# Sliding-window attention and a two-layer ELU network on one core: batch 1's queries and keys transposed in other portions and other steps

## The chip, the cores and the metric

The kernel runs on one core of a Trainium2 chip. The metric is the device time of one execution in microseconds (us). A core has five engines with a queue each, which work side by side and meet at semaphores: TensorE (PE, with its weight loads as PEld), VectorE (DVE), ScalarE (ACT), GpSimd (POOL) and SyncE (SP). POOL, SP and ACT also issue transfers to the DMA engines. TensorE writes its results to PSUM, a buffer of eight banks, from which DVE and ACT read them.

## The reference

Attention over 8 batches, 8 heads, 576 tokens and a head size of 64, in which a token sees only the tokens at most 32 away; then a network of two layers on the 4,608 tokens with 512 values each:

```python
scores = scale * np.matmul(q, k.transpose(0, 1, 3, 2))
scores = np.where(np.abs(pos[:, None] - pos[None, :]) <= 32, scores, -1e9)
attn = np.exp(scores - max); attn = attn / (sum(attn) + 1e-9)
x = np.matmul(attn, v)          # to (B*S, H*D) = (4608, 512)
h = x @ w_in                    # 512 x 2048
g = np.where(h > 0, h, np.exp(np.minimum(h, 0)) - 1)
out = g @ w_out                 # 2048 x 512, float32
```

## The kernel before

**The network's steps set the beat.** The 4,608 tokens are 18 tiles `t` of 256 tokens, and the 2,048 inner values are eight groups of 256, so there are 144 steps `kk`. The first 16 steps take tiles 0 and 1 in turn. In step `kk`, `mm1(kk)` makes `h` for one tile and one group: eight matmuls of 256 columns (L734, in the profile `ps`), with PSUM tiles in two banks, `h0` for even steps and `h1` for odd ones. `exponents` then issues the exp on ACT (L744, `e_sb`) and `subtract` the minus one on DVE (L756, `m_sb`). `elu(kk)`, issued on DVE at the start of step `kk + 1`, makes `g_sb` out of `ps` and `m_sb` (L767) and so frees the bank for step `kk + 2`. `mm2(n)` adds `g_sb` times `w_out` to the sums of a tile (four matmuls of 512 columns, L787, `psY`), for `n = kk - 2` in the general case. When a tile's last sums are done, ACT and DVE copy them out as `y_sb` and SP issues their transfer.

**Attention is laid between these by hand.** A dictionary of tasks holds what is issued in a step: `at(kk, slot, fn, ...)` enters it. A step runs its slots in the order "first", the `elu`, "dve", `mm1` (with "half" after its first four matmuls, before the exp is issued), "mid", the `mm2` (a slot with a number `n` runs just before `mm2(n)`), "end". Each engine takes its instructions strictly in the order in which they were issued.

**Pairs.** Attention is done for pairs of blocks of 64 queries, 36 pairs, four and a half to a batch. Pair 4 holds the last block of batch 0 and the first of batch 1; pair 5 is the next two blocks of batch 1, then 6, 7, and pair 8 its last two. `scores` (L384, into `psS`), `exponential` (ACT, L395, `pu`), `mask` (DVE, L404, `pm`), `pv` (L416), `normalize` (DVE, L425 and L428), `x_transpose` (L438) and `x_evac` bring a pair's result to `xT`, which `mm1` of tile `pair // 2` reads. Pair 4's scores come at the end of step 9, pair 5's in step 12, those of 6 and 7 in step 18, of 8 and 9 in step 26.

**Queries and keys must be transposed first**, heads and their 64 values onto the partitions, into `qT` and `kT` (two buffers each, batches in turn). A part of a batch is a pair `(z, nj)`: `32 * nj` tokens from token `z` on. Either `load_cast` brings it as bf16 by a POOL transfer that casts on the way (tile `c`), or `load_qk` brings float32 (tile `f`, SP) and `cast_qk` casts it (L290 on ACT, L292 on DVE, tile `qkb`). `transpose_qk` then transposes it on TensorE into a PSUM tile `ptx`: with `c`, two transposes of half the partitions for each of the `nj` (L335), with `qkb` one (L340); `evict` copies the result to `qT` or `kT`, with strides. From batch 3 on this is done by DMA.

In the kernel before, batch 1 comes in halves of 288 tokens: `HALF_A` by `load_cast`, transposed in steps 8 (queries) and 9 (keys); `HALF_B` by `load_qk`, cast in steps 14 (on ACT) and 15 (on DVE), transposed at the end of steps 15 and 16. The last 64 queries and 32 keys of batch 0 (`FRONT_C`) are transposed in step 6 by `transpose_late`. Batch 2 follows in four groups of nine in steps 22 to 25, which use the PSUM tiles "s" and "u" in turn; each of the two has two banks, and "s" and "u" hold the scores too. `HJ` is 9, `SJ` is 18 and `NC` is 32. ACT's copies of these groups, the casts, the exps and the copies of `xT` and `y_sb` share one queue.

Of the kernel before, what the change touches and what calls it, by code (L numbers as in the profile page):

```python
# [10 lines left out]
BF16 = mybir.dt.bfloat16  # L11
# [10 lines left out]
def kernel(  # L22
# [9 lines left out]
    nc = tc.nc  # L32

    B, H, S, D = q.shape
# [9 lines left out]
    HP = H // 2  # L44
    NC = 128 // HP
# [15 lines left out]
    cpool = ctx.enter_context(tc.tile_pool(name="const", bufs=1))  # L61
# [32 lines left out]
    def ps_tile(shape, dt, tag, name):  # L94
        return pools[tag].tile(shape, dt, tag=tag, name=name)
# [21 lines left out]
    HJ = SJ // 2  # L117
    WHOLE, HALF_A, HALF_B = (0, SJ), (0, HJ), (NC * HJ, HJ)
    FRONT_B = ((NC * HJ, HJ - 2), (NC * HJ, HJ - 1))
    FRONT_C = ((NC * (SJ - 2), 2), (NC * (SJ - 1), 1))  # L120
    qk_f = {}

    def load_qk(b, which, part, engs=(nc.sync, nc.sync)):
        z, nj = part
        mj = max(nj, HJ)
        t = lpool.tile([128, 2, mj * D], FP32, tag=f"f{which}{mj}",
                       name=f"f{which}", bufs=2 if part is WHOLE else 1)
        qk_f[b, which, z] = t
        src = (q, k)[which][b, :, z:z + NC * nj, :].rearrange(
            "(g h) (c j) d -> c g h (j d)", h=2, j=nj)  # L130
        for h in range(2):
            engs[h].dma_start(out=t[:, h, 0:nj * D], in_=src[:, :, h, :])
# [4 lines left out]
    def load_cast(b, which, part):  # L137
        z, nj = part
        mj = nj if nj < 3 else HJ + 1
        t = cpool.tile([128, 2, mj * D], BF16, tag=f"c{which}{mj}",  # L140
                       name=f"c{which}")[:, :, 0:nj * D]
        qk_c[b, which, z] = t
        src = (q, k)[which][b, :, z:z + NC * nj, :].rearrange(
            "(g h) (c j) d -> c g h (j d)", h=2, j=nj)
        nc.gpsimd.dma_start(out=t, in_=src)

    def load_v(b, m, rows=(0, 128)):
        lo = 128 * m - WIN
# [72 lines left out]
    def edges(i):  # L221
# [8 lines left out]
    ident = cpool.tile([128, 128], BF16)  # L230
# [15 lines left out]
        out=far, in_=far, compare_op=ALU.is_ge, fill=FAR,  # L246
# [61 lines left out]
    def keys_or_queries(b, which):  # L308
        if which == 0:
            return qT[b % 2].rearrange("p g s -> p (g s)")  # L310
        return kT[b % 2][:, KPAD:KPAD + HP * S]
# [233 lines left out]

    load_w_in(2, 0, 2)
    for which in range(2):
        load_cast(1, which, HALF_A)
    load_w_in(2, 1, 2)
    load_w_out(2)  # L550
    for m in range(3):
# [4 lines left out]
        load_v(1, m)  # L556
    gate(w_in_at(3))
    for which in range(2):
        load_qk(1, which, HALF_B)
    for which in range(2):  # L560
        load_qk(2, which, WHOLE)

# [5 lines left out]
    def at(kk, slot, fn, *args):  # L568
        tasks.setdefault((kk, slot), []).append((fn, args))
# [19 lines left out]
    at(1, "mid", x_transpose, 3, "y1")  # L589
    at(1, "mid", x_evac, 3, nc.vector)  # L590
    at(5, "dve", swap_pools)
    def transpose_late(tag):
        pt = ps_tile([128, 2, 512], BF16, tag, "ptx")
        evicts = []
        for which in range(2):
            transpose_qk(0, which, FRONT_C[which], 0, FRONT_C[which][1],
                         BOTH[which], later=evicts, pt=pt[:, which, :])
        for evict in evicts:
            evict()

    at(6, "mid", transpose_late, "s")
    at(6, "dve", rotate_back, 0, 3, 4, (1,))

    for which in range(2):
        at(8 + which, (6, "half")[which], transpose_qk, 1, which, HALF_A, 0,
           HJ, nc.scalar, "s")
        at(14 + which, "mid", cast_qk, 1, which, HALF_B, 0, HJ, BOTH[which])
        at(15 + which, "end", transpose_qk, 1, which, HALF_B, 0, HJ,
           nc.scalar, "s")
    at(6, "dve", edges, 2)  # L610
    at(16, "dve", hold_v, 2)
# [32 lines left out]
    for b in range(2, B):  # L644
        k0 = begin[first_pair(b)]


        l_qk, l_v, c0 = {2: (0, 0, 0), 3: (15, 24, 22), 4: (35, 36, 41),
                         5: (52, 52, 57), 6: (68, 68, 73),
                         7: (84, 84, 89)}[b]  # L650
        if b >= 3:
            at(l_qk, "end", load_qk, b, 0, WHOLE)
            at(l_qk, "end", load_qk, b, 1, WHOLE)
            if b > 3:
                at(l_v, "dve", hold_v, b)
            for m in range(VS):
                at(l_v + m, "mid", load_v, b, m)
        if b <= 3:

            if b == 2:  # L660
                at(k0, "dve", rotate_v, b, 0, 1)
            at((21, 28)[b - 2], "mid", rotate_v_dma, b, 3 - b)
        else:
            for n, back in enumerate((10, 8, 3, 2)):
                m0 = 2 * (n // 2)
                at(k0 - back, "dve", rotate_v, b, m0, m0 + 2, (n % 2,))
        if b == 2:

            for n, (which, j0) in enumerate(((0, 0), (0, 9), (1, 0), (1, 9))):
                at((18, 20, 21, 23)[n], ("mid", "end", "end", "mid")[n],  # L670
                   cast_qk, b, which, WHOLE, j0, 9,
                   (nc.vector, nc.scalar, nc.scalar, nc.vector)[n])
                at(22 + n, "end" if n == 1 else "mid", transpose_qk, b, which, WHOLE, j0, 9,
                   nc.scalar, "su"[n % 2])
            continue


        free = [f for f in range(c0, k0) if f not in starts]
        for n, (which, j0) in enumerate(
                (which, j0) for which in range(2) for j0 in (0, 6, 12)):  # L680
            at(free[n], "end", cast_qk, b, which, WHOLE, j0, 6,
               nc.vector if free[n] < 26 else nc.scalar)
            if j0 == 12:
                at(free[n], "end", write_rows, b, which)
                at(free[n] + (3 if free[n] == 29 else 4), "mid",
                   transpose_rows, b, which)
# [72 lines left out]
    def elu(kk, z=0):  # L759
        if z == 0:  # L760
            g_t[kk] = mpool.tile([128, FG, TT], BF16, tag="g_sb", name="g_sb",
                                   bufs=8)
        if kk == 0:
            subtract(kk, z)
        ps = psH[kk][z]
        w = ps.shape[1]
        nc.vector.scalar_tensor_tensor(  # L767
            g_t[kk][:, z * w:(z + 1) * w, :], ps, 0.0, m_t.pop((kk, z)),
            ALU.max, ALU.min)
# [69 lines left out]

    for kk in range(NSTEP):  # L840
        run(kk, "first")
        for n in {1: (), 2: (0, 1)}.get(kk, (kk - 1,)):
            if n >= 0:
                elu(n)
        run(kk, "dve")
        mm1(kk)
        run(kk, "mid")
        if kk == NSTEP - 1:
            last_sums()
        elif kk >= LATE + LAG:  # L850
            for _ in range(3 if kk < LATE + LAG + 4 else 4):
                add(*todo.pop(0))
        else:
            for n in {2: (), 3: (), 4: (), 5: (0, 2), 6: (1, 3), 7: (4,),
                      8: (5, 6)}.get(kk, (kk - LAG,) if kk >= LAG else ()):
                run(kk, n)
                mm2(n)
        run(kk, "end")
# [30 lines left out]
```

## Time and profile before

| what | value |
|---|---|
| three runs | 301.69, 302.32, 302.68 us; median 302.32 |
| the profiled execution | 302.52 us, of which span 300.8 us |
| TensorE's granted clock | 0.999 |
| TensorE busy | 97% of the span |
| DVE, ACT, POOL busy | 80%, 57%, 18% |
| DMA moved | 52.68 MB, 175 GB/s in the mean |
| step 6, products start | 23.87 us |
| step 10, products start | 35.05 us |
| step 19, products start | 54.52 us |
| step 26, products start | 69.92 us |

The span runs from the first instruction to the last; what the time has beyond it lies around the execution. Times within the profile count from the start of the span. In a timeline a matmul's length holds its way through the array, so lengths of matmuls that follow each other overlap; the distance of their starts is what they cost. A steady step takes 1.74 us: eight matmuls of `mm1` 0.87 and four of `mm2` 0.87.

### The profile page before, as it was taken

To read this page: it belongs to the slowest core of one execution; us is meant where nothing else is said; L and a number is where in the kernel's file an instruction comes from. 1 tells how busy PE (TensorE), PEld (TensorE's weight loads), DVE (VectorE), ACT (ScalarE), POOL (GpSimd) and SP (SyncE) were. 2 spreads that over 40 slices of the span, in tenths; PEclk is the share of its full clock that TensorE was granted. 3 is DMA by queue.
4 is the path that set the end of the run, shared out by engine and by line. 5 is a ranking of instruction groups with operands and counts; after the bars stand their busy time and mean duration, and the time that the engine had idled before them with its cause. 6 is when DMAs were issued, how large, how long until landed. Compare 5 with 4: busy or idle time off the path is not lost.

```text
span 300.8 us, 7664 instructions
## 1 busy us (share of the span) xinstructions
PE 291.8 (97%) x3066; PEld 198.6 (66%) x3118; DVE 240.9 (80%) x479; ACT 170.2 (57%) x258; POOL 52.7 (18%) x74
## 2 busy tenths in 40 slices
PE   7899999999999999999999999999999999999995
PEld 3585567677666666666666666666666666666673
DVE  7788588978787988888889789887988787877773
ACT  3783648688655567456745665467535353534342
POOL 8777203520005000410032002300000000000000
PEclk9999999999999999999999999999999999999999
DMA  9999999999957978999899989997921111111011
GB/s 190 168 200 203 185 233 349 370 179 231 241 159 199 239 116 270 244 267 135 161 256 323 172 203 252 312 153 137 268 54 72 35 72 38 70 37 70 2 70 71
DMA packets 94070, 52.68 MB, mean 175 GB/s; under 512 B 78163, under 2 KB 83795, under 8 KB 94035
## 3 DMA queue, kind: packets, MB, share of 16 engines
q1 hardware_dynamic: 47330, 35.61, 44.7%
q0 software_dynamic: 44976, 10.10, 44.2%
q10 hardware_dynamic: 1728, 6.49, 6.3%
q8 instruction: 24, 0.39, 0.6%
q14 instruction: 12, 0.09, 0.1%
HBM read 36.70 MB, written 15.34 MB: 173 GB/s over the span
## 4 chain that ended last, share of the span: by engine, by line
PE 85%; DMA 5%; issue 3%; DVE 2%; ACT 2%; POOL 2%; POOLq 0%; ACTq 0%; DVEq 0%
PE ps L734 39%; PE psY L787 38%; PE psS L416 4%; DMA out_dram<-y_sb 3%; PE psS L384 3%; DMA c<-in_k_dram 2%; ACT e_sb L744 1%; DVE g_sb L767 1%; PE ptx L335 1%; PE psXT L438 1%; POOL Vo L158 1%; DVE qkb L292 0%; ACT qkb L290 0%; PE ptx L340 0%; PE psS L364 0%
## 5 line engine op out<-in xcount | busy, mean ns | idle before, releaser
L744 ACT ACTIVATE e_sb<-ps 128x512 f32<-128x512 f32 (+1 forms) x145 | 86.3, 596 | 113.4 <-PE ps L734 106.0
L734 PE MATMUL ps<-xT,w_in_sb 128*128 128x256 bf16 (+1 forms) x1168 | 149.7, 271 | 0.1
L787 PE MATMUL psY<-w_out_sb,g_sb 128*128 128x512 bf16 (+2 forms) x541 | 139.3, 373 | 2.9 <-issue 0.3
L734 PEld LDWEIGHTS <-w_in_sb 128*128 128x128 bf16 x1168 | 110.4, 98 | 36.8 <-issue 0.8
L767 DVE SCALAR_TENSOR_TENSOR g_sb<-ps,m_sb 128x512 bf16<-128x512 f32 (+1 forms) x145 | 99.3, 686 | 13.1 <-DVE m_sb L756 0.5
L756 DVE TENSOR_SCALAR m_sb<-e_sb 128x512 bf16<-128x512 f32 (+1 forms) x142 | 61.5, 433 | 34.3 <-ACT e_sb L744 32.3
L787 PEld LDWEIGHTS <-g_sb 128*128 128x128 bf16 x592 | 55.9, 98 | 38.7
L151 POOL DMA_DIRECT2D Ve<-in_v_dram x37 | 32.5, 892 | 132.8 <-PE psS L416 79.5
L395 ACT ACTIVATE pu<-psS 128x1024 bf16<-128x1024 f32 x36 | 36.6, 1023 | 0.9 <-PE psS L384 0.8
L428 DVE TENSOR_TENSOR x_st<-psS,rc 128x512 bf16<-128x512 f32 x36 | 24.9, 692 | 1.2
L290 ACT CAST qkb<-f 128x768 bf16<-128x768 f32 (+1 forms) x29 | 25.0, 862 | 0.0
L404 DVE TENSOR_TENSOR pm<-pu,masks 128x1024 bf16<-128x1024 bf16 x32 | 21.8, 682 | 0.0
L416 PEld LDWEIGHTS <-pm 128*64 128x64 bf16 x512 | 9.6, 110 | 7.3 <-DVE pm L404 6.5
L292 DVE COPY y_sb<-psY 128x512 f32<-128x512 f32 (+1 forms) x18 | 12.2, 676 | 1.5 <-PE psY L787 1.5
L384 PEld LDWEIGHTS <-kT 64*128 64x128 bf16 x560 | 9.4, 95 | 4.6 <-issue 4.4
L290 ACT COPY y_sb<-psY 128x512 f32<-128x512 f32 (+1 forms) x19 | 10.8, 569 | 2.5 <-PE psY L787 2.5
L384 PE MATMUL psS<-qT,kT 64*128 64x64 bf16 x560 | 11.8, 191 | 0.1
L416 PE MATMUL psS<-Ve,pm 128*64 128x65 bf16 x288 | 11.5, 196 | 0.1
L290 ACT COPY qT<-ptx 128x1152 bf16<-128x1152 bf16 (+4 forms) x9 | 7.7, 882 | 5.0 <-PE ptx L340 3.5
L416 PE MATMUL psS<-Vo,pm 128*64 128x65 bf16 x224 | 10.3, 196 | 0.0
L175 DVE COPY Vo<-Ve 64x1040 bf16<-64x1040 bf16 (+1 forms) x22 | 9.1, 413 | 0.7
L425 DVE RECIPROCAL rc<-psS 128x8 f32<-128x8 f32 x36 | 7.2, 199 | 0.9 <-PE psS L416 0.9
(54 smaller groups left out, 91.3 us busy)
## 6 DMA issues: line engine op xcount, KB each, us to landing
out_dram<-y_sb SPq DMA_DIRECT2D x36, 256.0 KB, 3.5
f<-in_q_dram SPq DMA_DIRECT2D x12, 576.0 KB, 6.3
f<-in_k_dram SPq DMA_DIRECT2D x12, 576.0 KB, 8.0
in_dram<-qkb ACTq DMA_DIRECT2D x10, 576.0 KB, 4.2
Ve<-in_v_dram POOLq DMA_DIRECT2D x21, 128.0 KB, 12.6
w_out_sb<-in_moe_w_out_dram POOLq DMA_DIRECT2D x3, 512.0 KB, 10.4
Ve<-in_v_dram POOLq DMA_DIRECT2D x14, 96.0 KB, 11.6
w_in_sb<-in_moe_w_in_dram POOLq DMA_DIRECT2D x2, 512.0 KB, 10.4
```

Of the source, the lines that this page charges most:

```text
L151: nc.gpsimd.dma_start(out=V_e[b % 3][p0:p1, m, :, 0:D], in_=v[b, :, lo + p0:lo + p1, :].rearrange("h p d -> p h d"))
L290: nc.scalar.copy(d_, s_)
L384: nc.tensor.matmul(psS[:, h % 2, hp * 128 + z * QB:hp * 128 + (z + 1) * QB], lhsT=keys, rhs=qT[b % 2][base:base + 64, hp, QB * qb:QB * (qb ...
L395: nc.scalar.activation(pu, _bap(psS, [psS.ap[0], [1, 1024]]), AX.Exp, scale=SCALE)
L404: nc.vector.tensor_mul(pm, pu, _bap(mm, [mm.ap[0], [0, H], [1, 2 * QB]]))
L416: nc.tensor.matmul(psS[QB * z:QB * (z + 1), par, hp * VD:(hp + 1) * VD], lhsT=pm[:, par * HP + hp, z * QB:(z + 1) * QB], rhs=vv[:, qb // 2 ...
L428: nc.vector.tensor_mul(x_st, _bap(psS, [psS.ap[0], [VD, HP], [512, 2], [1, D]]), _bap(rc, [rc.ap[0], [2, HP], [1, 2], [0, D]]))
L734: nc.tensor.matmul(o, lhsT=w_in_sb[:, do, fo * 128:(fo + 1) * 128], rhs=r, start=(do == 0), stop=(do == NDO - 1))
L744: nc.scalar.activation(e_sb, ps, AX.Exp)
L756: nc.vector.tensor_scalar(m_sb, e_sb, -1.0, None, ALU.add)
L767: nc.vector.scalar_tensor_tensor(g_t[kk][:, z * w:(z + 1) * w, :], ps, 0.0, m_t.pop((kk, z)), ALU.max, ALU.min)
L787: nc.tensor.matmul(sum_of(t, ts, c), lhsT=g_t[n][:, j, ts * 128:(ts + 1) * 128], rhs=w_out_sb[:, s * FG + j, cols_of(c)], start=(s == 0 an ...
```

## The change

Batch 1 is cut anew. Its first part, `ONE_A`, is what pairs 4 and 5 read: 192 queries and 224 keys (`nj` 6 and 7). It is transposed together with `FRONT_C` in one group of 13 + 3 in step 8, just before `mm2(6)`, into one tile "s" of two banks; the four copies out of it go to DVE (queries of batch 1), ACT (keys of batch 1) and DVE (both of batch 0). `elu(8)` is issued ahead of that group, in step 8 rather than at the start of step 9. `transpose_late` and its group in step 6 are gone.

The second part, `ONE_B`, holds 256 queries and 256 keys (`nj` 8). Each is cast in two halves, one on ACT and one on DVE, in step 15 (queries) and 16 (keys), and transposed in the middle of the products of steps 16 and 17.

What is left, the last 128 queries and 96 keys of batch 1 (`LAST`), comes by two new POOL transfers in step 13, with the tokens on the partitions, held back until then by a small memset on DVE. `transpose_last` transposes them in step 22 behind batch 2's first group of nine, into the same tile "s", and copies them out on DVE ahead of ACT's copy of that group.

```diff
+    ONE_A = (0, 6), (0, 7)
+    ONE_B = tuple((NC * nj, HJ - 1) for _, nj in ONE_A)
+    LAST = tuple(S - z - NC * nj for z, nj in ONE_B)
...
+    def load_last(b, which):
+        nc.gpsimd.dma_start(
+            out=last[which].rearrange("p (h d) -> p h d", h=H),
+            in_=(q, k)[which][b, :, S - LAST[which]:S, :].rearrange("h p d -> p h d"))
+
+    def hold_last():
+        for which in range(2):
+            last[which] = cpool.tile([LAST[which], H * D], BF16,
+                                     name=f"last{which}")
+            nc.vector.memset(last[which][0:1, 0:2], 0.0)
+
+    def transpose_last(b, n, tag):
+        pt = ps_tile([128, 2048], BF16, tag, "ptx")
+        transpose_qk(b + 1, 0, WHOLE, 0, n, nc.scalar, later=(evicts := []),
+                     pt=pt[:, 0:n * 128])
+        los = n * 128, n * 128 + HP * LAST[0]
+        for which, lo in enumerate(los):
+            w = LAST[which]
+            for g in range(HP):
+                nc.tensor.transpose(
+                    pt[:, lo + g * w:lo + (g + 1) * w],
+                    last[which][:, 2 * g * D:2 * (g + 1) * D],
+                    ident[0:w, 0:w])
+        for which, lo in enumerate(los):
+            w = LAST[which]
+            nc.vector.tensor_copy(
+                keys_or_queries(b, which).rearrange(
+                    "x (g s) -> x g s", g=HP)[:, :, S - w:S],
+                pt[:, lo:lo + HP * w].rearrange("x (g s) -> x g s", g=HP))
+        for evict in evicts:
+            evict()
...
-        load_cast(1, which, HALF_A)
+        load_cast(1, which, ONE_A[which])
...
-        load_qk(1, which, HALF_B)
+        load_qk(1, which, ONE_B[which])
...
-    def transpose_late(tag):
-        pt = ps_tile([128, 2, 512], BF16, tag, "ptx")
-        evicts = []
-        for which in range(2):
-            transpose_qk(0, which, FRONT_C[which], 0, FRONT_C[which][1],
-                         BOTH[which], later=evicts, pt=pt[:, which, :])
+    def transpose_casts(tag):
+        pt = ps_tile([128, 2048], BF16, tag, "ptx")
+        n, evicts = 0, []
+        for b, parts, evacs in ((1, ONE_A, (nc.vector, nc.scalar)),
+                                (0, FRONT_C, (nc.vector, nc.vector))):
+            for which in range(2):
+                nj = parts[which][1]
+                transpose_qk(b, which, parts[which], 0, nj, evacs[which],
+                             later=evicts, pt=pt[:, n * 128:(n + nj) * 128])
+                n += nj
         for evict in evicts:
             evict()
 
-    at(6, "mid", transpose_late, "s")
+    at(8, 6, lambda: elu(8))
+    at(8, 6, transpose_casts, "s")
+    at(13, "dve", hold_last)
+    for which in range(2):
+        at(13, "mid", load_last, 1, which)
...
-        at(8 + which, (6, "half")[which], transpose_qk, 1, which, HALF_A, 0,
-           HJ, nc.scalar, "s")
-        at(14 + which, "mid", cast_qk, 1, which, HALF_B, 0, HJ, BOTH[which])
-        at(15 + which, "end", transpose_qk, 1, which, HALF_B, 0, HJ,
+        nj = ONE_B[which][1]
+        for n, eng in enumerate(BOTH):
+            at(15 + which, "mid", cast_qk, 1, which, ONE_B[which],
+               n * nj // 2, nj // 2, eng)
+        at(16 + which, "half", transpose_qk, 1, which, ONE_B[which], 0, nj,
            nc.scalar, "s")
...
-                at(22 + n, "end" if n == 1 else "mid", transpose_qk, b, which, WHOLE, j0, 9,
-                   nc.scalar, "su"[n % 2])
+                at(22 + n, "end" if n == 1 else "mid",
+                   *((transpose_last, 1, 9, "s") if n == 0 else
+                     (transpose_qk, b, which, WHOLE, j0, 9, nc.scalar,
+                      "su"[n % 2])))
...
-        for n in {1: (), 2: (0, 1)}.get(kk, (kk - 1,)):
+        for n in {1: (), 2: (0, 1), 9: ()}.get(kk, (kk - 1,)):
             if n >= 0:
                 elu(n)
```

More of the change, by code (lines that the diff above doesn't have):

```diff
@@ L145, in load_cast @@
         nc.gpsimd.dma_start(out=t, in_=src)
+    last = {}
+    def load_last(b, which):
[27 more added lines that the diff above has]
+            evict()
     def load_v(b, m, rows=(0, 128)):
```

## The prediction

> **What bounds the kernel now.** I read the page first (busy shares, chain), then the timeline of each engine from 20 to 80 us, where everything that the change touches lies, then the chain of waits there, and the groups by shape for durations. Of the page:
>
> ```profile
> PE 291.8 (97%) x3066; PEld 198.6 (66%) x3118; DVE 240.9 (80%) x479; ACT 170.2 (57%) x258; POOL 52.7 (18%) x74
> PE 85%; DMA 5%; issue 3%; DVE 2%; ACT 2%; POOL 2%; POOLq 0%; ACTq 0%; DVEq 0%
> ```
>
> TensorE works 97% of the span and the clock is 0.999, so time is won only by taking work off TensorE or by ending one of its few waits, and lost by each new wait: from step 26 on (69.92 us) nothing gives it back. Two places are close to a wait. In step 10 the matmuls of pv(4) follow the mask directly; in steps 22 to 25 the chain leaves TensorE and runs over ScalarE and VectorE. First the timeline (start, length, engine, line, what), then the chain (start, length, what):
>
> ```profile
> 33.41 1.12 ACT L290 COPY kT<-ptx 128x1152 bf16<-128x1152 bf16 x1 [0.91 <-PE ptx L335]
> 34.42 0.60 ACT L744 ACTIVATE e_sb<-ps 128x512 f32<-128x512 f32 x1
> 34.71 0.41 PE L384 MATMUL psS<-qT,kT 64*128 64x64 bf16 x16
> 35.15 1.02 ACT L395 ACTIVATE pu<-psS 128x1024 bf16<-128x1024 f32 x1
> 36.28 0.69 DVE L404 TENSOR_TENSOR pm<-pu,masks 128x1024 bf16<-128x1024 bf16 x1
> 37.03 0.34 PEld L416 LDWEIGHTS <-pm 128*64 128x64 bf16 x16 [0.56 <-DVE pm L404]
> ```
>
> ```profile
> 62.54 0.50 ACT e_sb L744
> 63.04 0.35 ACT qT L290
> ...
> 64.08 0.60 ACT xT L290
> 64.68 0.51 ACT e_sb L744
> ...
> 66.22 0.81 DVE qkb L292
> 67.04 0.59 DVE g_sb L767
> ```
>
> ```profile
> 65.41 1.04 PE L734 MATMUL ps<-xT,w_in_sb 128*128 128x256 bf16 x8
> 66.28 0.67 PE L340 MATMUL ptx<-ident,qkb 128*128 128x128 bf16 x9
> 67.68 1.03 PE L734 MATMUL ps<-xT,w_in_sb 128*128 128x256 bf16 x8
> ```
>
> The reader is to see that g_sb of step 23 ends at 67.63 and the products of step 25, which reuse its PSUM bank, start at 67.68: no slack. The xT copy ahead of it (64.08 to 64.68) feeds the products at 65.41, with 0.7 of slack.
>
> **What the Trainium skill says.** "PSUM — Partial Sum Buffer", section "PSUM bank collisions raise a hardware error": two engines may not touch one bank and quadrant at once, reads against reads included. The built order shows it obeyed: copies by different engines out of one bank wait for each other. Before has one such pair (late transposes: ACT copy at 25.44, DVE copy at 27.79), but DVE was busy until then, so its trace does not show the wait. "VectorE: DVE Perf Modes", section "Why PSUM operands drop a tier": a 16-bit PSUM source can still go twice as fast as 1x; the section on "Mode 2×_1P" adds that this wants neighbouring elements. The trace agrees: the rows below give 0.425 for a dense bf16 copy of 512, 0.698 for the strided one.
>
> ```profile
> L290 ACT COPY kT<-ptx 128x1152 bf16<-128x1152 bf16 x4 | 4.8, 1201 | 1.0 <-PE ptx L335 0.9
> L290 ACT COPY qT<-ptx 128x256 bf16<-128x256 bf16 x1 | 0.4, 368 | 0.0
> L290 ACT CAST qkb<-f 128x768 bf16<-128x768 f32 x26 | 21.6, 829 | 0.0
> L292 DVE COPY kT<-ptx 128x512 bf16<-128x512 bf16 x2 | 1.4, 698 | 0.1
> L292 DVE COPY xT<-psXT 128x512 bf16<-128x512 bf16 x2 | 0.8, 425 | 0.8 <-PE psXT L438 0.8
> L292 DVE COPY kT<-ptx 128x128 bf16<-128x128 bf16 x1 | 0.3, 282 | 0.0
> ```
>
> **A. Steps 6 to 10.** Removed: six transposes in step 6 (0.29), and groups of 18 in steps 8 and 9 (0.63 each with 0.08 of changeover). Added: one group of 32 in step 8; 18 take 0.63, so 0.035 each, 1.12. In step 6 the gain is cut: the products of step 8 start at 28.82 because elu(6) on DVE ends at 28.68, and DVE loses only the 0.20 that the small kT copy took between 27.79 and 27.99. So they start at 28.60, the second sums (0.87) at 29.47, the transposes at 30.42, and the last of them ends near 31.7 (30.42, 1.12 and some 0.2 in which a matmul drains). elu(8), now ahead of the copies, is done by about 31.5. The copies then go one after another over two engines, since they share banks: DVE queries of 768 strided (line through 0.282 and 0.698: 0.98), ACT keys of 896 (line through 0.368 and 1.12: 0.91), DVE 256 and 128 (0.42 and 0.28, 0.62 together), 0.05 for each hand-over: 34.35. TensorE is ready for scores(4) at 34.25 and starts it at about 34.42, before at 34.71. exp, mask and pv(4) keep their distance: scores to exp 0.44, exp 1.02, mask 0.69, two hand-overs, 2.25 in all (elu(9) no longer lies in between), so pv(4) at 36.67 instead of 37.03. **Gain 0.36**; bounds 0.1 (every copy 10% slower) and 0.6 (the copies wait for nobody). elu(9) is issued in step 10 in both kernels.
>
> **B. Steps 13 to 18.** Two memsets (0.06 each) on DVE in step 13 and two DMA issues of some 0.9 on POOL, which idles there for 16.8 us, cost nothing; behind the memsets stands mask(5), which ended 0.3 before pv(5). The two loads wait for the memsets, and batch 2's value loads stand behind them on POOL, held until 49.3 in any case; SP's order of issues stays as it was. The casts of the second part move from steps 14, 15 to 15, 16 and are halved over ACT and DVE, while the transposes go to the middle of the products of steps 16 and 17: 8 of 0.056 each instead of 9, **-0.1** in all, with 0.1 for two more changeovers. But now a cast has less than a step:
> - Queries: exp of step 15 starts at 46.52 (46.88 less 0.36), ACT's half cast of 512 (0.61 by the line through 0.829 and 1.15) ends at 47.6; DVE's, behind m_sb (47.16 to 47.55), at 47.95 to 48.2. TensorE gets there at 47.56 and takes the ACT half at once: **+0.25**.
> - Keys: on ACT stand the query copy of 1,024 (1.01, from 48.44), exp of step 16 (0.60) and the half cast (0.61), one behind the other: 50.5; m_sb and DVE's half end at 50.75 to 51.0. TensorE gets there at about 50.0: **+0.55**.
> Behind these on ACT stand a y_sb copy (0.60), the key copy (1.01) and exp(17); the keys are ready at 52.2 and scores(6) comes at 53.2. On DVE y_sb of the second tile follows later than the 52.57 of before, and scores(7) waits for it: **+0.1**. B is +0.8 (bounds 0, if the halves are done in time, and +1.2). A and B together: +0.45 at step 19.
>
> **C. Steps 22 to 25.** The last tokens add eight transposes (four of 128 columns, four of 96): 0.056 and 0.042 each, **+0.4** on TensorE. Their copies are dense: 0.425 and 0.36 on DVE, issued behind m_sb of step 22 (63.08, counted in the times of before) and ahead of the batch-2 cast and elu(22). They share a bank with the first nine transposes, so ACT's copy of these waits for them: it starts at 64.18 rather than 62.93, **1.25 late**. Behind it on ACT: xT(7) 65.36 to 65.95, exp(23) at 65.84 (before 64.55). TensorE, 0.42 later for its own work, is ready for step 24 at 65.83 and starts at 66.00: **+0.17**. From exp(23) to the end of elu(23) were 3.08 (64.55 to 67.63), so it ends at 68.92 and step 25 starts at 68.97 where TensorE is ready at 68.25: **+0.72**. Sum +1.3: 67.68 becomes 68.97. The rest of step 25 carries its old slack (products of step 26 start 0.9 after elu(24)), and no more is lost. Bounds: +0.4 (the copy's delay all in slack) and +1.9 (copies at the strided rate of 0.68 and 0.55).
>
> **DMA.** The cast loads shrink from 288 to 192 and 224 KB and four float loads from 288 to 256 KB, so the weights behind them land a little earlier, for which nobody waits. New are 1,024 and 768 rows of 256 bytes, issued near 41.8 and 43 while the float loads run. The value loads of the same form took 11.9 us in the median and 16.3 at most: landed by 54 to 59.5, wanted at 62. I take 0 for them. Batch 2's first cast wants its queries at 54.2; these landed by about 50.2.
>
> **Sum**: -0.36 + 0.8 + 1.3 = +1.7. The profiled execution took 302.52 (span 300.8 and 1.7 around it) and becomes 304.2; the median of 302.32 lies 0.2 below it, so 304.0. 0.3%, about 0.9 us, is what a measurement can tell from no change here.
>
> **Rivals.**
> - *The waits are covered* (chance 0.17). If the casts in steps 15, 16 are done when TensorE comes and the late ACT copy falls into slack, B is 0 and C is the eight transposes: -0.36 + 0.4 = 0.0, 302.3. ScalarE at 57% and 1.9 us less work there speaks for it; the zero slack at 67.68 against it. It decides on one mechanism, ACT's copy in step 22: if it starts less than about 0.4 late, no wait arises in step 25.
> - *Relief pays* (0.07): the same, and A at its upper bound with shorter waits for masks later on: -0.9 or a little more, 301.4. TensorE shows hardly a wait there to be shortened.
> - *The last rows come late* (0.12): the value loads issued at 49.66 landed only when the float loads were through (59.5). If the new rows share that fate, TensorE itself stands in step 22: +1.5 to 3 on top, 305.5 to 307.
> The order of the built kernel shows that the change does what it says.
>
> **Numbers.** The forecast has 0.64 and spans 303.2 (C at its lower bound) to 305.3 (all three at their worst); slower takes in the late rows: 0.76. Same 0.17, faster 0.07. Low end 302.2, which takes in the covered case, high end 305.4.
>
> **What would show it.** After: pv(4) some 0.3 us earlier against the products of step 6; the first transposes of steps 16 and 17 waiting for qkb; ACT's qT copy in step 22 starting over 1 us behind its exp with DVE's copies ahead of it; the products of step 25 waiting for g_sb. If step 19 comes no later than before, B is wrong; if the stretch from step 22 to 26 grows by 0.4 only, C is.

## The result, and the profile after

| | before | after |
|---|---|---|
| median of 10 runs each | 302.39 us (301.69 to 302.97) | 304.84 us (303.76 to 307.56) |
| ratio, 95% interval | 1 | 1.0084 [1.0057, 1.0111] |
| profiled execution, its span | 302.52, 300.8 us | 305.56, 303.8 us |
| products of step 6 to those of step 10 | 11.18 us | 10.24 us |
| step 10 to step 19 | 19.47 us | 21.02 us |
| step 22 to step 25 | 6.98 us | 8.36 us |
| step 26 to the end of the span | 230.88 us | 230.84 us |

The changed kernel is slower by 0.84%. The three stretches between steps 6 and 25 give -0.94, +1.55 and +1.38, together +2.0; 19 to 22 and 25 to 26 are as before, and so is everything after step 26. Ratios, here and below, are an estimate of their own without single executions that ran slow (over 1.5% above the fastest of their kernel), and not the quotient of the medians. This profiled execution also came to step 6 1.05 us later, because of a wait ahead of anything that the change touches (VectorE waited 1.8 us, until 7.74, for the first keys to land). A second profile of the same kernel, below, came to step 6 at 23.36 and has the same three differences.

The page first, the busy shares and the chain that ended last:

```profile
PE 295.1 (97%) x3114; PEld 198.2 (65%) x3114; DVE 242.8 (80%) x486; ACT 168.3 (55%) x257; POOL 53.3 (18%) x76
PE 92%; DVE 2%; DMA 2%; issue 2%; ACT 1%; SPq 0%; ACTq 0%; DVEq 0%
```

Nothing here tells that the kernel is slower: TensorE is at 97% as before, ScalarE even has less to do. The stages tell it.

**Steps 8 to 10**, timeline (start, length, engine, line, what, idle time before it and what ended that):

```profile
31.08 1.08 PE L376 MATMUL ptx<-ident,c 128*64 128x128 bf16 x32
32.21 0.96 DVE L333 COPY qT<-ptx 128x768 bf16<-128x768 bf16 x1
33.20 0.91 ACT L331 COPY kT<-ptx 128x896 bf16<-128x896 bf16 x1 [2.28 <-DVE qT L333]
34.14 0.42 DVE L333 COPY qT<-ptx 128x256 bf16<-128x256 bf16 x1 [0.97 <-ACT kT L331]
34.82 0.41 PE L425 MATMUL psS<-qT,kT 64*128 64x64 bf16 x16
37.14 0.33 PEld L457 LDWEIGHTS <-pm 128*64 128x64 bf16 x16 [0.57 <-DVE pm L445]
```

The copies run one after another over the two engines, each starting 0.03 us after the last one ends. They end at 34.76, TensorE comes to scores(4) at 34.7: it hardly waits. pv(4) follows its scores by 2.32, as before.

**Steps 16 to 18**, timeline:

```profile
49.61 5.14 POOL L192 DMA_DIRECT2D Ve<-in_v_dram  x6 [4.95 <-DVE Ve L211]
50.61 0.90 DVE L809 TENSOR_SCALAR m_sb<-e_sb 128x512 bf16<-128x512 f32 x1 [1.30 <-ACT e_sb L797]
51.14 0.40 PE L381 MATMUL ptx<-ident,qkb 128*128 128x128 bf16 x4 [0.37 <-ACT qkb L331]
51.90 0.40 PE L381 MATMUL ptx<-ident,qkb 128*128 128x128 bf16 x4 [0.37 <-DVE qkb L333]
54.97 0.41 PE L425 MATMUL psS<-qT,kT 64*128 64x64 bf16 x16 [0.15 <-DVE y_sb L333]
```

The eight key transposes fall into two groups of four, each waiting for its half of the cast. VectorE's half stands behind `m_sb` of step 16, which takes 0.90 us here and 0.43 in the median; POOL issues the value loads beside it.

**Steps 22 to 24**, the chain in order of time (start, length, what):

```profile
65.43 0.40 DVE qT L181
65.83 0.28 DVE kT L181
...
66.19 0.12 ACT qT L331
66.31 1.03 issue
67.34 0.60 ACT xT L331
67.94 0.04 issue
67.98 0.66 PE ptx L381 x9
```

and the same place in the timeline:

```profile
64.40 0.88 POOL L192 DMA_DIRECT2D Ve<-in_v_dram  x1 [2.33 <-PE ptx L175]
64.73 0.77 DVE L809 TENSOR_SCALAR m_sb<-e_sb 128x512 bf16<-128x512 f32 x1 [0.56 <-ACT e_sb L797]
66.19 1.29 ACT L331 COPY qT<-ptx 128x1152 bf16<-128x1152 bf16 x1 [1.49 <-DVE kT L181]
67.98 0.66 PE L381 MATMUL ptx<-ident,qkb 128*128 128x128 bf16 x9 [0.86 <-ACT xT L331]
```

ScalarE stands still for 1.49 us until VectorE's copies of the last tokens are through; its copy of `xT(7)` is queued behind; and TensorE, which wants the PSUM tile "u" that holds `xT(7)`'s transposes for batch 2's second group, waits 0.86 us. VectorE's copies are themselves late: `m_sb` of step 22, ahead of them, takes 0.77 us beside an issue of POOL, as that of step 16 does.

Of the groups by shape (busy time, mean ns, idle before), those that the prediction sized, and from the view of tile `last` how long its two loads took:

```profile
L331 ACT COPY qT<-ptx 128x1152 bf16<-128x1152 bf16 x2 | 2.6, 1289 | 1.7 <-DVE kT L181 1.5 <-PE ptx L381 0.3
L331 ACT CAST qkb<-f 128x512 bf16<-128x512 f32 x2 | 1.2, 620 | 0.0
L333 DVE COPY qT<-ptx 128x768 bf16<-128x768 bf16 x1 | 1.0, 957 | 0.0
L331 ACT COPY kT<-ptx 128x896 bf16<-128x896 bf16 x1 | 0.9, 905 | 2.3 <-DVE qT L333 2.3
```

```profile
DMA to landing us min/median/max: 17.9/18.9/20.0
```

### The profile page after: what moved, and what is told of

It is laid out like the page before. It is cut to its first block, busy times and chain, and to the rows that moved or that the text cites. A ratio compares the mean times of both kernels' runs of the same rounds, so it can differ in the third digit from the quotient of the medians.

```text
span 303.8 us, 7720 instructions
## 1 busy us (share of the span) xinstructions
PE 295.1 (97%) x3114; PEld 198.2 (65%) x3114; DVE 242.8 (80%) x486; ACT 168.3 (55%) x257; POOL 53.3 (18%) x76
## 4 chain that ended last, share of the span: by engine, by line
PE 92%; DVE 2%; DMA 2%; issue 2%; ACT 1%; SPq 0%; ACTq 0%; DVEq 0%
PE ps L787 41%; PE psY L840 40%; PE psS L457 4%; PE psS L425 4%; DMA f<-in_k_dram 2%; PE ptx L381 1%; PE psXT L479 1%; DVE qkb L333 1%; PE psS L405 0%; DVE x_st L469 0%; ACT e_sb L797 0%; ACT pu L436 0%; PE ptx L376 0%; PE ps_idle L520 0%; DVE pm L445 0%
## 5 line engine op out<-in xcount | busy, mean ns | idle before, releaser
L840 PE MATMUL psY<-w_out_sb,g_sb 128*128 128x512 bf16 (+2 forms) x592 | 147.4, 374 | 0.0
L192 POOL DMA_DIRECT2D Ve<-in_v_dram x37 | 31.5, 863 | 125.3 <-PE psS L457 79.9
L331 ACT CAST qkb<-f 128x768 bf16<-128x768 f32 (+2 forms) x30 | 25.0, 835 | 0.5 <-DMA f<-in_q_dram 0.5
L425 PE MATMUL psS<-qT,kT 64*128 64x64 bf16 x560 | 11.9, 191 | 0.5 <-DVE kT L333 0.3
L381 PE MATMUL ptx<-ident,qkb 128*128 128x128 bf16 x70 | 6.0, 232 | 3.5 <-DVE qkb L333 2.2
L331 ACT COPY qT<-ptx 128x512 bf16<-128x512 bf16 (+4 forms) x7 | 6.1, 904 | 4.9 <-PE ptx L381 3.4
```

The source lines that it names most:

```text
L192: nc.gpsimd.dma_start(out=V_e[b % 3][p0:p1, m, :, 0:D], in_=v[b, :, lo + p0:lo + p1, :].rearrange("h p d -> p h d"))
L331: nc.scalar.copy(d_, s_)
L425: nc.tensor.matmul(psS[:, h % 2, hp * 128 + z * QB:hp * 128 + (z + 1) * QB], lhsT=keys, rhs=qT[b % 2][base:base + 64, hp, QB * qb:QB * (qb ...
L840: nc.tensor.matmul(sum_of(t, ts, c), lhsT=g_t[n][:, j, ts * 128:(ts + 1) * 128], rhs=w_out_sb[:, s * FG + j, cols_of(c)], start=(s == 0 an ...
```

## The experiments

**The theory**: the loss has two places, (B) the late, halved key cast, and (C) VectorE's copies of the last tokens, which hold ScalarE in step 22; the last rows are a third danger. **The rivals**: the changed kernel is slow because TensorE has more to do (eight transposes, more groups), or the lost time only comes back behind the next late thing. The readings below are of three stretches in one profile per kernel, and the two of the changed kernel differ by up to 0.16 in one of them; before has 11.18, 19.47 and 6.98.

| kernel | median us | ratio to before | 6 to 10 | 10 to 19 | 22 to 25 |
|---|---|---|---|---|---|
| changed, again | 304.53 | 1.0071 [1.0056, 1.0085] | 10.40 | 21.02 | 8.31 |
| e1 casts early | 303.57 | 1.0044 [1.0029, 1.0058] | 10.58 | 19.73 | 11.33 |
| e2 own banks | 304.87 | 1.0081 [1.0062, 1.0101] | 10.34 | 21.44 | 8.20 |
| e3 both of these | 303.33 | 1.0044 [1.0025, 1.0062] | 10.43 | 19.73 | 8.99 |
| e4 last rows early | 304.00 | 1.0055 [1.0043, 1.0067] | 10.29 | 20.83 | 8.01 |
| e5 copies after | 303.39 | 1.0045 [1.0035, 1.0055] | 10.28 | 21.02 | 7.48 |
| e6 first part alone | 302.70 | 1.0019 [1.0004, 1.0035] | 10.52 | 20.98 | 6.94 |
| e7 e1, e4 and e5 | 303.16 | 1.0022 [1.0006, 1.0037] | 10.37 | 20.48 | 7.34 |
| e8 keys on DVE, e4 and e5 | 302.27 | 1.0000 [0.9983, 1.0018] | 10.54 | 19.74 | 7.34 |
| e9 keys on DVE | 303.29 | 1.0039 [1.0023, 1.0056] | 10.61 | 19.93 | 8.28 |
| e10 values later | 303.81 | 1.0061 [1.0041, 1.0082] | 10.69 | 20.53 | 8.04 |
| e11 first part, e9's casts | 302.91 | 1.0029 [1.0016, 1.0042] | 10.24 | 20.99 | 6.94 |

The kernel before had medians of 302.06 to 302.25 beside them; the first four rows, e4 to e7, e8 to e10 and e11 come from four chips. The 21.44 of e2 holds a wait of 0.45 for weights that the others do not have.

**e1_casts_early**: the casts whole again, in steps 14 and 15, all else as changed.

```diff
-        for n, eng in enumerate(BOTH):
-            at(15 + which, "mid", cast_qk, 1, which, ONE_B[which],
-               n * nj // 2, nj // 2, eng)
+        at(14 + which, "mid", cast_qk, 1, which, ONE_B[which], 0, nj,
+           BOTH[which])
```

> The changed kernel with one thing undone: batch 1's second part is cast whole in steps 14 (queries, ACT) and 15 (keys, DVE), as before the change; its transposes stay in steps 16 and 17. Theory (late casts make TensorE wait in steps 16 and 17, 1.0 us in the profile of the changed kernel, and push the copies behind them): the two waits for qkb vanish, the stretch from the products of step 10 to those of step 19 falls from 21.0 to about 19.6 us, the time from 304.8 to about 303.5. Rival (the loss is the DMA's: new rows of 256 bytes slow the other loads): the waits for the casts are then waits for the loads behind them and stay; 304.8.

Step 10 to 19 took 19.73: the waits for `qkb` are gone. But its profiled execution, the slowest of its 18 (306.54 us), shows the third danger. Timeline, then the windows (start and end, length, TensorE's busy time; its granted clock is the third number from the right):

```profile
64.25 0.47 PE L175 MATMUL ptx<-ident,last 96*128 96x96 bf16 x4 [2.16 <-DMA last<-in_k_dram]
```

```profile
62.00:64.30 2.30, 0.14 (x3) 0.05 (x2) 0.56 (x2) 0.66 (x2) 0.00 (x0) 1.00 2.36 168
64.30:66.30 2.00, 2.00 (x9) 0.90 (x10) 1.54 (x4) 0.77 (x1) 0.91 (x2) 0.51 4.29 116
66.30:68.10 1.80, 1.80 (x14) 1.46 (x13) 0.28 (x1) 1.09 (x2) 1.45 (x2) 0.60 4.82 86
68.10:70.00 1.90, 1.85 (x20) 1.37 (x19) 1.05 (x3) 0.97 (x2) 0.18 (x1) 1.00 4.40 116
```

TensorE stood 2.16 us for the last keys, which landed 21 us after their issue, and then ran at half its clock for 3.4 us (0.50 from 64.30 to 67.70). So the casts are worth 1.3 us in their stretch, and a TensorE that comes earlier meets the last rows.

**e2_own_banks**: of batch 2's first group only eight transposes (one bank of tile "s"), so that the last tokens have the other bank for themselves; ten in the second group.

```diff
+                t0, nt = ((0, 8), (8, 10), (0, 9), (9, 9))[n]
-                   *((transpose_last, 1, 9, "s") if n == 0 else
-                     (transpose_qk, b, which, WHOLE, j0, 9, nc.scalar,
+                   *((transpose_last, 1, 8, "s") if n == 0 else
+                     (transpose_qk, b, which, WHOLE, t0, nt, nc.scalar,
```

> The changed kernel with one thing changed: in step 22 batch 2's first group has 8 transposes instead of 9 and the second 10, so the first fills one PSUM bank and the last tokens of batch 1 lie wholly in the other. ACT's copy then no longer waits for DVE's two copies; all work stays. Theory (the shared bank strings the copies one behind the other): ACT's copy starts within 0.2 us of the end of its exp instead of 1.6 us after its start, the 0.9 us wait in step 23 vanishes, the stretch from the products of step 22 to those of step 25 falls from 8.36 to about 7.4 us, the time to about 303.8. Rival (the late landing of the last rows, or ACT's own queue, sets that stretch): no change, 304.8.

It did not take the wait away:

```profile
65.55 1.03 ACT L331 COPY qT<-ptx 128x1024 bf16<-128x1024 bf16 x1 [1.35 <-DVE kT L181]
67.11 0.72 PE L381 MATMUL ptx<-ident,qkb 128*128 128x128 bf16 x10 [0.55 <-ACT xT L331]
```

ScalarE's copy still starts when VectorE's end, though they read different banks. So it is not the bank that orders the two engines here. What is left in common is the PSUM tile, whose readers seem to go in the order of issue. As a test of what the wait costs, e2 says nothing.

**e3_both**: the edits of e1 and e2 together.

> Both edits together: casts whole in steps 14 and 15, and banks of their own in step 22. Theory: the two add up, since each removes its own wait: about 1.3 and 1.0 us less than the changed kernel, so 302.5, level with the kernel before; what is left is eight more transposes (0.4 us) against the gain in steps 6 to 10. Rival (one wait only covers another one behind it): no more than the better of the two alone, 303.5.

19.73 again in step 10 to 19. Batch 2's second group waits no longer, but only since TensorE already stood 1.48 us in step 22 for the last keys (no drop of the clock followed here):

```profile
63.47 0.34 PE L175 MATMUL ptx<-ident,last 96*128 96x96 bf16 x4 [1.48 <-DMA last<-in_k_dram]
```

The median, 303.33, is hardly below e1's 303.57, as the rival had it.

**after_again**: the changed kernel once more, on the chip of e1 to e3.

> The changed kernel itself on the chip of the others, for comparison: 304.8 us by all theories. What differs between executions is the landing of the last 96 key rows, which came 0.2 us ahead of need in its profile: if these rows set the time in some executions, its times spread further (303.8 to 307.6 so far) than those of the kernel before (301.7 to 303.0).

304.53 us; 21.02 and 8.31 in the stretches, with the same wait of 0.81 for `xT`. The differences in the profile repeat.

**e4_last_early**: memsets and loads of the last rows in step 9, not 13.

```diff
-    at(13, "dve", hold_last)
+    at(9, "dve", hold_last)
...
-        at(13, "mid", load_last, 1, which)
+        at(9, "mid", load_last, 1, which)
```

> The changed kernel with the memsets and the two loads of the last rows moved from step 13 to step 9; nothing else. Theory (in the changed kernel the waits in steps 16, 17 and 23 set the time and the rows land just ahead of need): the rows land some 8 us earlier, no execution waits for them; the median stays near 304.5, the times spread less, and m_sb of step 13 is no longer slowed by POOL's issue. Rival (the rows' landing sets the time of many executions): the median falls by 0.5 or more.

The two loads, now issued some 4 us ahead of the float loads and not among them, land 10.0 and 10.1 us after their issue instead of 17.9 and 20.0. The median is 304.00; 22 runs lie within 303.49 to 304.75, where the changed kernel's first ten went up to 307.56 (its second six only to 304.77). That is 0.53 below after_again, which the rival asked for, but not for its reason: no profile of the changed kernel waits for the rows. The three stretches are 0.60 shorter than in after_again, 0.48 of it in two places where `m_sb` has no issue of POOL beside it any more: in step 13 (0.43 for 0.72; step 15 is 0.19 shorter) and in step 22 (the wait for `xT` is 0.52 for 0.81):

```profile
63.78 0.43 DVE L809 TENSOR_SCALAR m_sb<-e_sb 128x512 bf16<-128x512 f32 x1 [0.56 <-ACT e_sb L797]
```

**e5_copies_after**: VectorE's two copies of the last tokens issued after `elu(22)` in step 23 (and ScalarE's copy ahead of them), nothing else.

```diff
+        for evict in evicts:
+            evict()
+        last["pt"] = pt
+
+    def copy_last(b, n):
+        pt = last["pt"]
...
-        for evict in evicts:
-            evict()
...
+    at(23, "dve", copy_last, 1, 9)
```

> The changed kernel with DVE's two copies of the last tokens moved behind elu(22), to the head of step 23, and issued after ACT's copy of batch 2's first group out of the same tile; the work is the same. Theory (ACT's copy, waiting for DVE's two, pushes the xT copy and with it the transposes of step 23): ACT's copy starts right after its exp, the wait of 0.8 us in step 23 is gone, products of step 22 to products of step 25 take about 7.5 us instead of 8.3, the time falls from 304.5 to about 303.7. Rival (the late landing of the last rows holds TensorE anyway): the wait moves to the last rows' transposes and the time stays within 0.3.

```profile
64.35 1.29 ACT L336 COPY qT<-ptx 128x1152 bf16<-128x1152 bf16 x1
66.27 0.41 DVE L188 COPY qT<-ptx 128x512 bf16<-128x512 bf16 x1
66.86 0.67 PE L386 MATMUL ptx<-ident,qkb 128*128 128x128 bf16 x9
```

ScalarE's copy follows its exp without idle time, and TensorE's second group follows the products without a wait. Step 22 to 25 falls by 0.88 to 7.48, the median by 1.1 us against after_again, beside a kernel before of the same median. C is shown, and with it what e2 failed to show. Of the 0.5 us left over before, the eight transposes are 0.36 (what e7 and e8 keep); for the rest TensorE waited, since the last keys landed at 63.80 and their transposes began at 63.85.

**e6_first_part_alone**: only part A; the rest of batch 1, 12 and 11 times 32 tokens, as a second part with casts in steps 14 and 15 and no last rows (in tiles of the size of the later batches). The main lines, against the changed kernel:

```diff
-    ONE_B = tuple((NC * nj, HJ - 1) for _, nj in ONE_A)
+    ONE_B = tuple((NC * nj, SJ - nj) for _, nj in ONE_A)
...
+        at(14 + which, "mid", cast_qk, 1, which, ONE_B[which], 0, nj,
+           BOTH[which])
+        at(15 + which, "end", transpose_qk, 1, which, ONE_B[which], 0, nj,
```

> Only the first half of the change: batch 1's first part (6 and 7) and batch 0's end in one group in step 8, with elu(8) ahead; all the rest of batch 1 (12 and 11 groups of 32 tokens) comes as in the kernel before, float32, cast whole in steps 14 and 15, transposed at the ends of steps 15 and 16; no last rows. The casts and loads of batch 1 take their buffers from the pair that later batches use. Theory (the gain of the change lies in steps 6 to 10, some 0.6 to 0.9 us, and all loss behind them): products of step 6 to those of step 10 take 10.3 us instead of 11.2, five more transposes of 0.056 in steps 15 and 16 cost 0.3, so about 0.5 below the kernel before: 301.8. Rival (the gain in steps 6 to 10 is only time lost earlier, given back): 302.3 to 302.6.

A's gain is there (10.52) and step 22 to 25 is as before, but step 10 to 19 takes 20.98, 1.51 more than before. Five more transposes are some 0.28 of it (0.056 each); the largest part is a wait that neither kernel shows:

```profile
45.88 1.47 ACT L294 CAST qkb<-f 128x1536 bf16<-128x1536 f32 x1 [1.05 <-DMA f<-in_q_dram]
47.89 0.83 PE L344 MATMUL ptx<-ident,qkb 128*128 128x128 bf16 x12 [0.87 <-ACT xT L294]
```

**e7_all_undone**: the edits of e1, e4 and e5 together.

> Three edits to the changed kernel together: casts whole in steps 14 and 15, the last rows loaded in step 9, DVE's copies of them behind elu(22). Theory (three waits, each removed by its edit, and they add up): no wait for qkb, none for the last rows, none for xT in step 23; what is left is the gain of steps 6 to 10 (0.6 to 0.9) against eight transposes (0.4) and some changeovers: 302.0 to 302.4, level with the kernel before. Rival (something else in the new cut costs time, such as the copies out of one tile in step 8): 303 or more.

Above what was expected by 0.8 us, and for the same reason, with TensorE waiting 0.59 us for `xT`:

```profile
45.88 1.04 ACT L336 CAST qkb<-f 128x1024 bf16<-128x1024 f32 x1 [1.20 <-DMA f<-in_q_dram]
```

The float load of the queries is issued at 38.5 to 40.0 in all kernels, behind a gate on the weights, whatever TensorE has gained by then, and has landed 4.6 to 7.0 us later: at 44.1 in e1, at 45.8 in e6 and e7. Before, ScalarE comes to the cast at 45.36, only 0.15 after the landing; with A's gain it comes at 44.7 and finds it landed (e1 and e3) or not (e6 and e7), and `xT(5)` is queued behind. This need not be chance: with the last rows loaded in step 9 (e4, e7, e8) the landing took 6.5 to 7.0 us, with the larger second part (e6, e11) 6.5 and 6.7, in the eight other profiles of the changed kernel and its variants 4.6 to 6.0. The cast in step 15 never waits for it.

**e8, e9, e10**: the queries as in the changed kernel; the keys whole on VectorE, at the end of step 15, into 1.3 us in which it idles (e8 and e9). e9 is the changed kernel with that edit alone, e8 has e4's and e5's too. e10 is the changed kernel with the value loads held until step 18.

```diff
+        if which:
+            at(15, "end", cast_qk, 1, which, ONE_B[which], 0, nj, nc.vector)
-        for n, eng in enumerate(BOTH):
+        for n, eng in enumerate(() if which else BOTH):
```

```diff
-    at(16, "dve", hold_v, 2)
+    at(18, "dve", hold_v, 2)
...
-        at(16 + m, "mid", load_v, 2, m)
+        at(18, "mid", load_v, 2, m)
```

> The changed kernel with one edit: batch 1's keys (second part) cast whole on DVE at the end of step 15, not in halves on ACT and DVE in step 16. Theory: the two waits of 0.37 us, the split of the transposes and the wait of scores(7) for y_sb go; step 10 to 19 falls from 21.02 to 19.7 to 20.0 us, all else as in the changed kernel (step 22 to 25 at 8.3); median 0.9 to 1.3 lower, 303.2 to 303.7. Rival (the stretch is long because TensorE has more to do or the query side waits): 20.7 or more, median above 304.2.

> The changed kernel with batch 2's value loads held and issued in step 18, not from step 16 on. Theory (POOL's issuing beside it makes DVE's multiplication m_sb of step 16 take 0.90 instead of 0.43 us, and with it the key half cast late): m_sb(16) takes 0.43; the two waits for qkb add up to 0.3 instead of 0.74; step 10 to 19 falls by 0.3 to 0.5 to 20.5 to 20.7; median 304.0 to 304.3. Rival (the 0.90 is ACT's own e_sb or a bank, not POOL): m_sb(16) still at 0.7 to 0.9 and the stretch at 21.0.

> Batch 1's second part: queries cast as in the changed kernel (halves on ACT and DVE in step 15), keys cast whole on DVE at the end of step 15, into DVE's idle 1.3 us ahead of the step-16 multiplication; last rows issued in step 9; DVE's copies of the last tokens after elu(22). Theory (the whole loss sits in the key cast's wait, the late last rows and the copies that hold ACT; the query cast must not be earlier than step 15, because its float load lands at about 45.8 us whatever TensorE does): no wait for qkb, for xT or for the last rows above 0.2 us; stretch from the products of step 10 to those of step 19 at 19.6 to 19.9 us, step 22 to 25 at 7.3 to 7.5, step 6 to 10 at 10.3 to 10.4; median 302.0 to 302.5, level with before. Rival (the lost time comes back behind the next late thing, as in the run with everything undone): 303.0 or more, with a wait of 0.4 us or more still in steps 13 to 18.

In e9 the keys are transposed in one group and without a wait, and both scores follow in one:

```profile
49.50 0.61 PE L381 MATMUL ptx<-ident,qkb 128*128 128x128 bf16 x8
52.33 0.85 PE L425 MATMUL psS<-qT,kT 64*128 64x64 bf16 x32
```

Step 10 to 19 falls by 1.09 to 19.93, the median to 303.29. In e10 `m_sb` of step 16 takes 0.43 again, and one of the two waits is left:

```profile
49.17 0.43 DVE L809 TENSOR_SCALAR m_sb<-e_sb 128x512 bf16<-128x512 f32 x1 [1.43 <-ACT e_sb L797]
49.70 0.68 PE L381 MATMUL ptx<-ident,qkb 128*128 128x128 bf16 x8 [0.38 <-ACT qkb L331]
```

Step 10 to 19 falls by 0.49: that is the share of the value loads' issue in B. e8 came out at 302.27, level with before. No wait for the keys' cast, `xT` or the last rows is left, and 0.2 us for the queries' cast (step 16 takes 2.37 for 2.18 in e1); of its transposes in steps 16, 17 and 22:

```profile
46.90 0.69 PE L386 MATMUL ptx<-ident,qkb 128*128 128x128 bf16 x8
49.16 0.61 PE L386 MATMUL ptx<-ident,qkb 128*128 128x128 bf16 x8
...
61.21 0.56 PE L175 MATMUL ptx<-ident,last 128*128 128x128 bf16 x8
```

Its three stretches sum to 37.62 us, those of before to 37.63: A's gain is then just spent on the second part's additional 0.27 and the last tokens' 0.36. One more wait is left, of 0.24 us at scores(4), which the view puts down to the memset in step 9:

```profile
29.41 0.85 DVE L817 TENSOR_SCALAR m_sb<-e_sb 128x512 bf16<-128x512 f32 x1 [0.46 <-ACT e_sb L805]
33.57 0.41 PE L430 MATMUL psS<-qT,kT 64*128 64x64 bf16 x16 [0.24 <-DVE last L163]
```

But e4 and e7 have the same memset and no such wait, and e1 waits 0.27 there without it. What e1 and e8 share is `m_sb` of step 8, which took 0.88 and 0.85 beside an issue of POOL, so that the copies began late.

**e11_first_part_and_casts**: as e6, with the casts of e9 and the transposes in the middle of steps 16 and 17. It asks whether A pays once the casts are right and the last tokens need not be moved.

> Only part A of the change (batch 1's first 6 and 7 tokens in one group with batch 0's end, in step 8), the rest of batch 1 (12 query and 11 key tokens, so no last rows) as a second part whose query cast lies in step 15 in halves on ACT and DVE and whose key cast is whole on DVE at the end of step 15, transposes in the middle of steps 16 and 17. Theory (A alone is worth about 0.65 us, the second part costs nothing when no cast is early enough to wait for its load nor late enough to hold the transposes, and batch 2 is untouched): no wait for xT or qkb above 0.2 us in steps 13 to 18, step 6 to 10 at 10.5, step 10 to 19 at 19.5 to 20.0, step 22 to 25 at 6.95; median 0.2 to 0.8 below before. Rival (a longer second part keeps ACT too long: its copies of 12 and 11 tokens at 1.4 us each hold the elu behind them, so products or scores in steps 17 to 19 wait by 0.3 us or more): step 10 to 19 at 20.2 or more, median level with before or above.

The rival was right. The casts wait for no load, but ScalarE's copies of 12 and 11 times 32 tokens take 1.44 and 1.33 us, the exps behind them are late, and so is VectorE's copy of `y_sb`:

```profile
50.69 1.33 ACT L294 COPY kT<-ptx 128x1408 bf16<-128x1408 bf16 x1
53.93 0.41 PE L388 MATMUL psS<-qT,kT 64*128 64x64 bf16 x16 [0.55 <-DVE y_sb L296]
```

20.99 in step 10 to 19, 302.91 us. The last tokens in batch 2's first group buy a shorter second part, 19.74 against 20.99, for 0.36 there; left in it, they cost more. No version faster than before was found.

## Why the prediction was right, point by point

The direction and the range held: 304.84 for 304.0. The sum was +1.7 against +2.0 in the profiles, and the medians lie 2.45 and 2.28 apart. That the sum came so close is in part luck: A brought 0.58 more than predicted and B cost 0.75 more. The stretches of after_again explain 2.1 of the medians' distance; what lies above stays open. Executions in which the last rows land late would explain it, but no profile of the changed kernel shows one, and e6, which has no such rows, has single executions up to 307.64 too.

- **A was under-sized**: 0.36 predicted, 0.94 in the profile, 0.49 to 0.94 in the thirteen profiles that hold A. The copies ran strung on one another and took the time worked out (0.96 and 0.91 against 0.98 and 0.91). Two terms failed. The wait for `elu(6)`, taken as staying, went in this profile: `g_sb` ended at 28.99, products at 29.25, and steps 6 and 7 took 4.33 for a predicted 4.73. In e9 and e10 it stayed, with 0.21 and 0.29, and there A brought 0.57 and 0.49. The other is the start of scores(4): from the group of 32 to the next products lay 1.02, not the 1.22 that the prediction's times hold, and the last transpose drained in 0.06, not 0.2, so TensorE and the copies met and hardly one waited. Steps 8 and 9 took 5.91 for a predicted 6.16. They did so in ten of the thirteen; in after_again, e1 and e8 `m_sb` of step 8 met an issue of POOL, and they took 6.06, 6.23 and 6.20.
- **B was mis-sized**: +0.8 predicted, +1.55 measured, outside its bounds. Queries: +0.25 predicted, 0.2 measured (step 16 took 2.38, and 2.18 in e1 with its early cast), in waits too short for the view to print. Keys and scores(7): +0.55 and +0.1 predicted, e9 shows 1.09 to be had back. The term that failed is VectorE's half behind `m_sb` at its usual 0.43; it took 0.90, and e10 shows that the value loads' issue does this and costs 0.49 of the stretch. The 0.6 left is what was predicted. I had these loads on POOL's queue in view, as held "until 49.3 in any case", but only for POOL's order, not for what they do to VectorE. The same failed in step 13: the issues of the last rows were to cost nothing, but `m_sb` took 0.73 beside them, the transposes of `xT(5)` came late, and step 15 took 2.15 (1.96 in e4). The terms also add up to 0.9, not 0.8, if the 0.1 for changeovers is counted; e1 shows no changeover (eight transposes amid the products took 0.45).
- **C was right in size, by luck in part, and wrong in place**: +1.3 predicted, +1.38 measured. The eight transposes made step 22 longer by the predicted 0.4, and that is all that the rival of more work for TensorE is worth. ScalarE's copy came 1.60 later behind its exp than before, for a predicted 1.25; in e4, where `m_sb` of step 22 took 0.43 and not 0.77, it came 1.26 later, and the stretch was 8.01 and not 8.36. The rest came as one wait of 0.86 at batch 2's second group and not as 0.17 and 0.72 at the products of steps 24 and 25. The prediction gave the copy of `xT(7)` 0.7 of slack, up to the products at 65.41; the group that wants its tile began in the kernel before 0.22 behind the copy's end (64.68):

```profile
64.90 0.67 PE L340 MATMUL ptx<-ident,qkb 128*128 128x128 bf16 x9
```

  e5 took the wait away alone.
- **The banks were the wrong reason for C.** The Trainium skill, "PSUM — Partial Sum Buffer", section "PSUM bank collisions raise a hardware error", has it that two engines may not touch one bank and quadrant at once, and was read as the cause of the copies' order. e2 has that order without a shared bank, so it does not come from there alone.
- **DMA was wrong and cost little by luck**: the last rows, estimated from the value loads' 11.9 us in the median, took 17.9 and 20.0 us and landed at about 63.9, where TensorE wanted the keys at 63.9. In e1, e3 and e10 TensorE came earlier and stood for 2.16, 1.48 and 0.53 us, in e5 and e9 for 0.13. The rival *last rows late* was not what set the median, but it is real.
- *The waits are covered* and *relief pays* fell with ScalarE's copy, as the prediction said: it was over 1 us late, and a wait arose, if in another place.

## What to carry to other kernels

Moving work later is priced by what stands ahead of it on each queue at that moment, and by what other engines do to those instructions: here a cast with half a step less of slack met an instruction that took twice its time. Issuing a transfer on POOL is work that VectorE may feel: by an estimate from e10 and e4 (0.49, 0.19 and 0.35), three such meetings, in steps 16, 13 and 22, make up about 1.0 of the 2.9 us that B and C cost. Before two copies by different engines are put on one PSUM tile, ask who is queued behind the second; issued in the other order, in e5, they held nobody up. And a gain ahead of a transfer with a fixed time of issue can be lost at that transfer: look up how close its first reader stands to its landing.

## What the runs showed of the hardware

- `m_sb` (float32 to bf16 in SBUF, 128x512) takes 0.43 us, and more only beside an issue of POOL. In the fourteen profiles it ran 1,694 times with no issue beside it and took at most 0.44 us. It began 66 times in the middle of an issue (at least 0.24 us after the issue's start and 0.25 before its end): it then took 0.48 to 0.90 us each time and ended 0.22 to 0.26 us after the issue did. Begun in the first 0.23 us of an issue (125 times) it kept its 0.43. `g_sb`, which reads PSUM, took no more than 0.69 us in the 171 times that it began in the middle of one. The Trainium skill, "SBUF — State Buffer", section "SBUF: two separate sides", has VectorE and GpSimd share a pair of ports under an exclusive lock, for some of VectorE's operations only; whoever starts first holds it for a whole instruction. The wait up to the issue's end fits that; that the first 0.23 us of an issue hold nothing back is not stated there. No run here tells a lock from another cause on POOL's side.
- Two loads in rows of 256 bytes, 1,024 and 768 of them, took 9.3 to 10.1 us when issued some 4 us ahead of the float loads (e4, e7, e8). Issued among them they took 15 to 21 us in seven profiles, and 4.9 and 10.7 in e2.
- After TensorE stood 2.16 us (e1), its clock was 0.50 for 3.4 us; after 1.48 us (e3) it stayed at 1.00. The Trainium skill, "TensorE: Matmul & The Clock Gate", section "What's actually happening", puts the half clock behind an idle window of about 3.4 us; here a shorter stand was followed by it, in one profile.
